# One 2 KB-row transfer for two blocks' filters, and a new table of places, in a long-convolution and SwiGLU kernel

## The chip, the core and the metric

The kernel runs on one core of a Trainium2 chip. The core has TensorE (PE, matmuls; its weight loads are shown as PEld), VectorE (DVE), ScalarE (ACT), GpSimd (POOL) and SyncE (SP, which here only issues transfers). They run side by side; each takes its own instructions strictly in the order in which the program issued them, and waits on semaphores for the others and for DMA transfers. The metric is the device time of one execution in microseconds.

## The reference

The sequence has 2048 rows of D = 640 channels, the feed-forward width is F = 1728, and everything is bf16 at the boundary.

```python
def _A_ref(q, k, v, shift_k, ssm_k, ssm_D):
    k_pad = jnp.pad(k, ((0, 0), (ks - 1, 0), (0, 0)))          # ks = 4
    for t in range(ks):                                        # four taps per channel
        k_shift = k_shift + k_pad[:, t:t + S, :] * shift_k[:, ks - 1 - t][None, None, :]
    kv = k_shift * v
    kv_f = rfft of kv over time, padded to 2 * S
    kf_f = rfft of ssm_k over time, padded to 2 * S            # ssm_k is (D, S)
    y = irfft(kv_f * kf_f)[:S]                                 # a causal convolution per channel
    y = y + kv * ssm_D[None, None, :]
    return q * y

def _B_ref(x, w_gate, w_up, w_down):
    return (silu(x @ w_gate) * (x @ w_up)) @ w_down

x = A_q
h = x + _A_ref(_layernorm(x), A_k, A_v, A_shift_k, A_ssm_k, A_ssm_D)
out = h + _B_ref(_layernorm(h), B_w_gate, B_w_up, B_w_down)
```

The fences above shorten the transforms to words.

## The kernel before

**Blocks.** Time is cut into NB = 4 blocks of BLK = 512 rows. Each block's piece of the filter `ssm_k` (called g) and of kv is carried into a spectrum by matmuls with a fixed basis (`forward`, weights WF). Spectra are called G0 to G3 and X0 to X3; each is of size "S" (two arena units: two halves `h` of four planes). From the G of a block and of the one before, `window` makes H (H0 = G0). The output spectrum A of block j is the sum of X_i times H_(j-i) over i = 0 to j (`mac`), so block 3 has four complex products, and an inverse transform (`inverse`, weights WI) brings it back to time. There follow the two layer norms, a transpose of the normalized rows (`turn_h`), and the feed-forward part (`ffn`): 13.5 chunks of 128 columns, gate and up projections of five matmuls each (`proj`, L769), Silu and products into `tT` (L783 to L787), and the down matmuls (L845). In the program of the order below, block j's convolution lies beside block j-1's feed-forward.

**mac in detail.** Where block j has more than one product, MODE is "one": each complex product needs four products of 128x2560 on VectorE (L542). Two of them are added into a buffer `acc`, two into the halves of A (through `plus`, L545). `acc` is one buffer, so its additions come one after the other. At the end come a subtraction and an addition (L581, L582), and then the inverse's own preparation (L662, L663, and L674, L677).

**Memory.** Blocks of 128 x 2560 bf16 live in an arena of 22 units of 5 KB per partition. A unit is given out at a buffer's first use and taken back after its last; a buffer of size 2 takes an even unit and its neighbour.

**What sets the order.** Every step is recorded as a numbered operation with an engine and its dependences, and then issued in the sequence of the table ORDER. A negative entry (the complement of the number) takes the operation's other form: an eviction of PSUM (L319, L413) goes to VectorE instead of ScalarE; a transfer from HBM (`load`) is issued from Pool's queue instead of SP's; an addition made by `added` is done not by VectorE but by an accumulating DMA that Pool issues (L243, the destination is read, added to and written by the transfer); the up half of a gate is read from PSUM directly by VectorE. Since buffers and arena units are given out in this sequence too, the table also sets which waits there are.

**g.** `load_g` brings the 512 time steps of one block, for 640 channels, as 128 x 5 x 512: rows of 1 KB. For block 0 the transposes are made by PE (L411) out of the loaded buffer; for blocks 1 to 3 ScalarE first rearranges the buffer by a copy (L419, 128x2560), and four transposing transfers from SP (L404) turn it.

The lines that the prediction speaks of:

```python
    def added(ns, fn, to, what, reads, write, n=1):
        plan.add("dve", ns, fn, reads, [write], ("add", 2 * P * R * D * n, lambda: nc.gpsimd.dma_start(out=to(), in_=what(), accum_op=ALU.add, max_dma_last_dim=4 * D)))
...
            dve(1402, lambda: v.tensor_sub(A.part(0), A.part(0), A.part(1)), [A.at(1)], [A.at(0)])
            dve(1402, lambda: v.tensor_add(A.part(1), total(), parts[1][0]()), [acc, parts[1][1]], [A.at(1)])
...
    act(400, lambda: nc.scalar.activation(ap(junk)[:, 0, 0:1], ap(bn)[:, 0, 0:1], ACT.Silu), [(bn, 0)], [])
```

The last of these (L871) is a Silu of one column, whose result isn't used; it is the first Silu of the program.

Of the kernel before, what the change touches and what calls it, by code (L numbers as in the profile page):

```python
# [16 lines left out]
D = 640  # L17
FF = 1728
P = 128
BLK = 512  # L20
NB = S_TOT // BLK
R = BLK // P
L = 2 * BLK
EPS = 1e-5
KT = D // P
# [166 lines left out]
def kernel(ctx: ExitStack, tc: tile.TileContext, A_q, A_k, A_v, A_shift_k, A_ssm_k, A_ssm_D, B_x,  # L192
# [21 lines left out]
    def new(kind):  # L214
        return Buf("U", kind, None, 2 if kind == "S" else 1) if kind in views else Buf(kind, kind)
# [66 lines left out]
    MB = P * R * D * 2  # L282
# [4 lines left out]
    def load_g(j):  # L287
        b = new("ld")
# [702 lines left out]
```

## Time and profile before

| | before |
|---|---|
| median of 3 runs | 251.36 us (251.21 to 253.07) |
| profiled execution: span | 251.4 us |
| TensorE busy | 237.3 us (94%) |
| VectorE busy | 197.7 us (79%) |
| ScalarE busy | 173.9 us (69%) |
| Pool busy | 54.0 us (21%) |
| bytes moved by DMA | 33.66 MB, mean 134 GB/s |
| accumulating transfers (L243) | 11 |

The profiled execution's own time is its span, 251.4 us; nothing lies outside of it. Busy time is the sum over an engine's instructions without the waits. A row of the chain of waits is start, length and what ran; a row of a timeline adds in brackets how long the engine was idle before it and who released it. In a row of windows, after the length, the engines stand in the order PE, PEld, DVE, ACT, POOL, each with busy time and count; then PE's granted clock, the share of the DMA engines that was busy, and GB/s.

### The profile page before, as it was taken

What the parts mean: (1) busy time and instruction counts of PE and PEld (TensorE: products, weight loads), DVE (VectorE), ACT (ScalarE), POOL (GpSimd) and SP (SyncE); (2) the same over time, 40 slices, a digit from 0 to 9 for tenths busy, and PEclk for the clock granted to TensorE, in tenths of its full rate; (3) what the DMA queues carried; (4) which work ended last, traced back from release to release, by engine and by line L of the source; (5) the groups of instructions that cost most, each with busy time, mean ns of one, the idle gap of its engine ahead of it and who ended that gap; (6) DMA issues with size and microseconds to landing.
All of it is one profiled execution on the core that took longest, in us unless ns stands there. A gap on an engine that the chain in (4) does not pass through costs nothing.

```text
span 251.4 us, 5138 instructions
## 1 busy us (share of the span) xinstructions
PE 237.3 (94%) x2113; PEld 153.0 (61%) x2125; DVE 197.7 (79%) x249; ACT 173.9 (69%) x300; POOL 54.0 (21%) x54
## 2 busy tenths in 40 slices
PE   3869997999999999999999999999999999999994
PEld 3447675788777677444465676454456785465662
DVE  2379999999999999999999989999999542131222
ACT  2449998999999976975988789983542865325100
POOL 0002003231540313220270404263612110000030
PEclk9999999999999999999999999999999999999999
DMA  5995699774998654685345468889592200000052
GB/s 156 376 212 163 127 324 352 231 197 92 165 246 292 202 81 81 105 154 133 79 66 146 86 99 194 148 146 163 98 224 29 26 0 3 0 0 3 0 78 78
DMA packets 37283, 33.66 MB, mean 134 GB/s; under 512 B 22470, under 2 KB 32076, under 8 KB 37260
## 3 DMA queue, kind: packets, MB, share of 16 engines
q1 hardware_dynamic: 31884, 21.38, 32.1%
q0 software_dynamic: 5376, 11.96, 25.9%
q8 instruction: 16, 0.26, 0.4%
q14 instruction: 7, 0.06, 0.1%
HBM read 16.29 MB, written 4.59 MB: 83 GB/s over the span
## 4 chain that ended last, share of the span: by engine, by line
PE 56%; ACT 17%; DMA 10%; DVE 9%; issue 4%; SPq 3%; DVEq 0%; ACTq 0%; POOLq 0%
PE ps L769 24%; PE ps L845 22%; ACT arena L319 7%; DMA arena<-in_A_ssm_k_dram 7%; PE ps L698 5%; DMA arena<-arena 3%; ACT sg L785 2%; PE ps L490 2%; SPq L404 2%; ACT junk L606 1%; PE ps L329 1%; PE ps L833 1%; DVE arena L674 1%; DVE arena L663 1%; DVE arena L662 1%
## 5 line engine op out<-in xcount | busy, mean ns | idle before, releaser
L769 PE MATMUL ps<-arena,wgu 128*128 128x512 bf16 (+1 forms) x668 | 116.7, 328 | 1.4 <-ACT sg L809 0.5
L769 PEld LDWEIGHTS <-wgu 128*128 128x128 bf16 x680 | 66.2, 98 | 45.3 <-issue 1.4
L845 PE MATMUL ps<-wd,tT 128*128 128x320 bf16 x416 | 59.1, 299 | 0.0
L845 PEld LDWEIGHTS <-tT 128*128 128x128 bf16 x416 | 39.8, 98 | 17.2 <-issue 1.8
L542 DVE TENSOR_TENSOR arena<-arena 128x2560 bf16<-128x2560 bf16 x30 | 44.1, 1484 | 0.2
L783 ACT ACTIVATE sg<-ps 128x1024 bf16<-128x1024 f32 (+1 forms) x28 | 26.9, 968 | 20.3 <-PE ps L769 19.7
L329 PE MATMUL ps<-arena,WF 128*128 128x320 bf16 x176 | 29.8, 299 | 1.2 <-ACT arena L319 0.9
L785 ACT CAST sg<-ps 128x1024 bf16<-128x1024 f32 (+1 forms) x23 | 23.0, 998 | 6.9 <-PE ps L769 3.1
L319 ACT CAST arena<-ps 128x320 bf16<-128x320 f32 (+1 forms) x48 | 25.2, 583 | 1.9 <-DVE arena L545 1.1
L610 POOL TENSOR_TENSOR sm<-sm,neghalf 128x4 f32<-128x4 f32 (+1 forms) x10 | 16.6, 1659 | 43.4 <-DVE sm L646 43.1
L787 DVE TENSOR_TENSOR tT<-sg,sg 128x1024 bf16<-128x1024 bf16 (+1 forms) x23 | 15.5, 673 | 11.5 <-ACT sg L785 11.5
L243 POOL DMA_DIRECT2D arena<-arena x11 | 13.3, 1211 | 47.4 <-DVE arena L542 11.2
L329 PEld LDWEIGHTS <-WF 128*128 128x128 bf16 x176 | 17.1, 98 | 10.0 <-issue 2.3
L606 ACT ACTIVATE junk<-arena 128x640 bf16<-128x640 bf16 x28 | 20.8, 744 | 1.3 <-DVE arena L709 1.3
L545 DVE TENSOR_TENSOR arena<-arena 128x2560 bf16<-128x2560 bf16 x14 | 20.7, 1487 | 0.2
L319 ACT ACTIVATE arena<-ps 128x640 bf16<-128x640 f32 (+1 forms) x32 | 20.2, 655 | 0.3
L698 PE MATMUL ps<-arena,WI 128*128 128x320 bf16 x96 | 15.7, 299 | 0.9 <-issue 0.6
L850 ACT ACTIVATE row<-ps,sm 128x640 bf16<-128x640 f32 x12 | 9.5, 791 | 8.2 <-PE ps L845 8.0
L709 DVE SCALAR_TENSOR_TENSOR arena<-arena,sm,ps 128x640 bf16<-128x640 bf16 x16 | 13.6, 876 | 1.8 <-ACT ps L707 1.8
L852 POOL DMA_DIRECT2D out_dram<-row x12 | 11.7, 1153 | 14.1 <-ACT row L850 14.1
L707 ACT ACTIVATE ps<-ps,sm 128x640 f32<-128x640 f32 x16 | 12.1, 770 | 3.7 <-PE ps L698 3.5
L698 PEld LDWEIGHTS <-WI 128*128 128x128 bf16 x96 | 9.0, 97 | 5.6 <-issue 1.3
(91 smaller groups left out, 240.8 us busy)
## 6 DMA issues: line engine op xcount, KB each, us to landing
arena<-arena POOLq DMA_DIRECT2D x11, 640.0 KB, 6.1
arena<-in_A_q_dram SPq DMA_DIRECT2D x4, 640.0 KB, 5.1
out_dram<-row POOLq DMA_DIRECT2D x13, 160.0 KB, 4.2
arena<-in_A_ssm_k_dram SPq DMA_DIRECT2D x3, 640.0 KB, 9.4
arena<-in_A_v_dram SPq DMA_DIRECT2D x3, 640.0 KB, 6.3
wd<-in_B_w_down_dram SPq DMA_DIRECT2D x2, 800.0 KB, 7.3
out_dram<-arena POOLq DMA_DIRECT2D x2, 640.0 KB, 5.8
wgu<-in_B_w_gate_dram SPq DMA_DIRECT2D x1, 800.0 KB, 6.5
```

The lines of the kernel that those rows point to most:

```text
L319: (lambda: nc.scalar.activation(dst(), src(), ACT.Copy, scale=2.0)) if twice else (lambda: nc.scalar.copy(dst(), src())),
L329: nc.tensor.matmul(ap(ps)[:, h, 0:NH], w, ap(src)[:, r, h * NH:(h + 1) * NH], start=(first and i == 0), stop=(last and i == len(rs) - 1), ...
L542: dve(1402, lambda: v.tensor_mul(to(), X.part(xs), H.part(hs)), [X.at(xs), H.at(hs)], [at])
L545: added(1402 * n - 69 * (n - 1), lambda: v.tensor_add(to(), to(), b()), to, b, [what], at, n)
L606: act(725, lambda r=r: nc.scalar.activation(waste(), ap(x)[:, r, :], ACT.Square, scale=D ** -0.5, accum_out=sm(s, MSQ, (r,))), [(x, r)], [ ...
L610: nc.gpsimd.tensor_tensor(sm(s, RSTD, rs), sm(s, VAR, rs), ap(neghalf)[:, 0:len(rs)], op=ALU.pow)
L698: nc.tensor.matmul(ap(ps)[:, w, 0:NH], m, src[:, w * NH:(w + 1) * NH], start=(i == 0), stop=(i == len(terms) - 1))
L769: nc.tensor.matmul(split(ap(ps), n)[:, i, :], w(k), ap(hT)[:, k, lo:lo + n], start=(k == 0), stop=(k == KT - 1))
L783: act(905 if wide_ else 490, lambda: nc.scalar.activation(of(sg), of(*gate), ACT.Silu), [(gate[0], gate[1] + i) for i in range(m)] + (psu ...
L785: op = plan.add("act", 905 if wide_ else 490, lambda: nc.scalar.copy(of(co), of(*up)), psu + [sg], [co] + tt, ("dve", 1135 if wide_ else 6 ...
L787: op.rest = dve(602 if wide_ else 336, lambda: nc.vector.tensor_mul(to(), of(sg), of(co)), [sg, co], tt)
L845: nc.tensor.matmul(ap(ps[hf])[:, hf, 0:NH], ap(tT)[:, c * BLK + at:c * BLK + at + P], ap(wd)[:, c, hf * NH:(hf + 1) * NH], start=False, st ...
```

## The change

`load_g(0)` now brings the g of blocks 0 and 1 in one transfer of 128 x 5 x 1024, whose rows are 2 KB, into a buffer of the new kind "pair", two neighbouring arena units. It returns a list of two pieces, each a buffer and a view of its half; block 1 takes the second piece and loads nothing. `g_turned` reads through that view. There is one operation fewer, so the numbers behind it shift by one, and the whole table ORDER is another.

```diff
-    0, 1, 2, 3, 16, 18, -20, 5, 4, 8, 17, 186, 9, 20, 22, 7, 10, 11, -22, 24, -26, 23, 26, 75, 76, 13, 15, 12, 6,
...
+    8, 16, 17, 26, 0, 1, 3, 9, 18, 19, 20, 10, 24, 7, 11, 5, -26, 22, 21, -24, 75, 12, 192, 6, 76, 36, 77, 78, 79,
...
+             "pair": ("p (c t) -> p c t", {"c": KT}), "scr": ("p (a d) -> p a d", {"a": 4}), "hT": ("p (k t) -> p k t", {"k": KT}),
...
-        return Buf("U", kind, None, 2 if kind == "S" else 1) if kind in views else Buf(kind, kind)
+        return Buf("U", kind, None, 2 if kind in ("S", "pair") else 1) if kind in views else Buf(kind, kind)
...
     def load_g(j):
-        b = new("ld")
-        load(MB, lambda q: q.dma_start(
-            out=ap(b).rearrange("p (c t) -> p c t", c=KT),
-            in_=A_ssm_k[0:D, j * BLK:(j + 1) * BLK].rearrange("(c p) t -> p c t", p=P)), [b])
-        return b
+        n = 2 if j == 0 else 1
+        b = new("pair" if n > 1 else "ld")
+        def at(i=0):
+            t = ap(b) if n > 1 else ap(b).rearrange("p (c t) -> p c t", c=KT)
+            return t[:, :, i * BLK:(i + 1) * BLK]
+        load(n * MB, lambda q: q.dma_start(
+            out=ap(b) if n > 1 else at(),
+            in_=A_ssm_k[0:D, j * BLK:(j + n) * BLK].rearrange("(c p) t -> p c t", p=P)), [b])
+        return [(b, lambda i=i: at(i)) for i in range(n)]
...
-    def g_turned(g, j):
+    def g_turned(loaded, j):
+        g, g_at = loaded
...
             act(2414, lambda: nc.scalar.copy(ap(by_r).rearrange("q a b -> q (a b)").rearrange("q (r c p) -> q r c p", r=R, c=KT),
-                                             ap(g).rearrange("q (c p r) -> q r c p", c=KT, r=R)), [g], [by_r])
+                                             g_at().rearrange("q c (p r) -> q r c p", r=R)), [g], [by_r])
...
-    gT = g_turned(g, 0)
+    gT = g_turned(g[0], 0)
...
-        g = load_g(j)
+        g = g[1:] or load_g(j)
...
-        gT = g_turned(g, j)
+        gT = g_turned(g[0], j)
```

What the table moves is seen in what each engine issues. At the start of the program SP and Pool issue the loads. SP before (`in_A_ssm_k_dram` is g, first of block 1, then of block 0; `in_A_q_dram` is x):

```order
L477 DMA arena<-in_A_k_dram 128x1280
L889 DMA arena<-in_A_shift_k_dram 5x512
L477 DMA arena<-in_A_k_dram 128x1280
L289 DMA arena<-in_A_ssm_k_dram 128x5x512
L296 DMA arena<-in_A_v_dram 128x2560
L903 DMA WF<-const_wf 128x1024
L904 DMA arena<-in_A_ssm_D_dram 1x640
L289 DMA arena<-in_A_ssm_k_dram 128x5x512
L903 DMA WF<-const_wf 128x1024
L301 DMA arena<-in_A_q_dram 128x2560
```

Pool before issued no transfer there. Now SP has these, the last a transpose of block 1's g that waits for ScalarE's copy:

```order
L895 DMA arena<-in_A_shift_k_dram 5x512
L483 DMA arena<-in_A_k_dram 128x1280 x2
L301 DMA arena<-in_A_v_dram 128x2560
L294 DMA arena<-in_A_ssm_k_dram 128x5x1024
L409 DMA_TRANSPOSE arena<-arena 128x5x128
```

and Pool, behind the identity matrix, these:

```order
L878 AFFINE_SELECT ident<-ident 128x128
L909 DMA WF<-const_wf 128x1024
L910 DMA arena<-in_A_ssm_D_dram 1x16x40
L306 DMA arena<-in_A_q_dram 128x2560
L909 DMA WF<-const_wf 128x1024
L752 DMA wd<-in_B_w_down_dram 128x3x640
L915 DMA WI<-const_wi 128x1024
L301 DMA arena<-in_A_v_dram 128x2560
L755 DMA wd<-in_B_w_down_dram 64x640
L294 DMA arena<-in_A_ssm_k_dram 128x5x512
```

The pair stands fifth on SP, and WF, x and others have moved to Pool's queue, beside it. ScalarE's first instructions before (L419 is the copy of block 1's g, L319 an eviction of block 0's first transform):

```order
L871 ACT_TABLE_LOAD
L871 ACTIVATE junk<-bn 128x1
L413 COPY kT<-ps_75 128x5x128
L419 COPY arena<-arena 128x2560
L413 COPY arena<-ps_73 128x640
L319 ACTIVATE arena<-ps_72 128x320
```

and now (L425 is the copy, L324 the eviction, L877 the Silu of one column):

```order
L418 ACT_TABLE_LOAD
L418 COPY kT<-ps_73 128x5x128
L418 COPY kT<-ps_74 128x5x128
L425 COPY arena<-arena 128x2560
L324 ACTIVATE arena<-ps_74 128x320
L877 ACT_TABLE_LOAD
L877 ACTIVATE junk<-bn 128x1
L324 ACTIVATE arena<-ps_75 128x320
```

The Silu stands behind the first eviction, with a second table load of its own, and the eviction of a g transpose (L413, 128x640) is gone from ScalarE. The third place is Pool's queue in block 3, ahead of its inverse, with the semaphores waited for (a DMASW one is a transfer that Pool issued, a DMAHW one a transfer of SP). Before, with the load of v and one layer norm's small work between:

```order
L243 DMA arena<-arena 128x2x1280 [waits DMASW4_49,DMASW2_49,DVE_49]
L243 DMA arena<-arena 128x2x1280 [waits DMASW5_49,DVE_49]
L243 DMA arena<-arena 128x2x1280 [waits DVE_49]
...
L243 DMA arena<-arena 128x2x1280 [waits DMASW5_49]
L243 DMA arena<-arena 128x2x1280 [waits DMASW3_49,DMASW0_49,DVE_49]
L852 DMA out_dram<-row_68 128x640 [waits DMAHW4_49,DMASW1_49]
L243 DMA arena<-arena 128x2x1280 [waits DMASW6_49,DVE_49]
```

Now (L858 adds a row of the feed-forward's result to the output; a second such row is left out):

```order
L243 DMA arena<-arena 128x2x1280 [waits DMASW5_49,DVE_49,PE_49]
L243 DMA arena<-arena 128x2x1280 [waits DMASW6_49,DVE_49]
L243 DMA arena<-arena 128x2x1280 [waits DMASW7_49,DMASW5_49]
L858 DMA out_dram<-row_67 128x640 [waits DMASW0_49,Activation_49]
L243 DMA arena<-arena 128x2x1280 [waits DMAHW5_49,DMAHW6_49,DMAHW1_49,DMAHW7_49,DMAHW0_49,DMASW1_49]
L243 DMA arena<-arena 128x2x1280 [waits DMASW6_49,DMASW2_49,DVE_49]
L243 DMA arena<-arena 128x2x1280 [waits DMAHW2_49,DMAHW3_49,DMASW7_49,DMASW3_49]
...
L243 DMA arena<-arena 128x2x1280 [waits DMASW3_49,DVE_49]
L243 DMA arena<-arena 128x2x1280 [waits DMASW1_49,DVE_49]
L243 DMA arena<-arena 128x2x1280 [waits DMASW5_49]
L243 DMA arena<-arena 128x2x1280 [waits DMASW6_49,DMASW0_49,DVE_49]
L243 DMA arena<-arena 128x2x1280 [waits DMASW7_49,DVE_49]
```

Eleven accumulating transfers stand where six stood, all eleven behind the spectrum G3; five of them wait for an earlier one's landing on `acc`. In the whole program there are 25 instead of 11, and VectorE has 14 additions fewer. On VectorE the addition L588 (L582 before) now waits for the last of the eleven, and two products into tT (L793), L668, L669 and L680 (L662, L663, L674 before) stand around and behind it ahead of block 3's inverse.

More of the change, by code (lines that the diff above doesn't have):

```diff
@@ L201 @@
     views = {"x": ("p (r d) -> p r d", {"r": R}), "t4": ("p (r d) -> p r d", {"r": R}), "ld": (None, None), "early": (None, None),
-             "scr": ("p (a d) -> p a d", {"a": 4}), "hT": ("p (k t) -> p k t", {"k": KT}),
+             "pair": ("p (c t) -> p c t", {"c": KT}), "scr": ("p (a d) -> p a d", {"a": 4}), "hT": ("p (k t) -> p k t", {"k": KT}),
              "minus": ("p (a q) -> p a q", {"a": 5}), "S": ("p (h a d) -> p h a d", {"h": 2, "a": 4})}
@@ L425, in g_turned @@
             for r in range(R):
-                transposed(lambda c, r=r: ap(g).rearrange("q (c p r) -> q c p r", c=KT, r=R)[:, c, :, r], [g],
+                transposed(lambda c, r=r: g_at().rearrange("q c (p r) -> q c p r", r=R)[:, c, :, r], [g],
                            lambda r=r: ap(gT)[:, r, :].rearrange("p (c q) -> p c q", c=KT), (gT, r))
```

82 rows, old and new, of the table ORDER are left out of this document.

## The prediction

> **What bounds the kernel now.** I read the page first, then the windows, the chain of waits, and single groups.
>
> ```profile
> span 251.4 us, 5138 instructions
> PE 237.3 (94%) x2113; PEld 153.0 (61%) x2125; DVE 197.7 (79%) x249; ACT 173.9 (69%) x300; POOL 54.0 (21%) x54
> ```
>
> TensorE (PE) is busy in all but 14.1 us. The windows say where those lie (length, then busy time of PE, PEld, VectorE, ScalarE, Pool, then PE's granted clock, DMA share, GB/s).
>
> ```profile
> 0.00:5.00 5.00, 1.00 (x11) 0.80 (x12) 0.42 (x3) 1.49 (x2) 0.54 (x6) 1.00 0.52 153
> 5.00:10.00 5.00, 4.91 (x130) 3.62 (x129) 2.23 (x8) 1.28 (x2) 0.00 (x0) 1.00 0.89 317
> 10.00:15.00 5.00, 2.02 (x36) 0.83 (x35) 3.15 (x6) 1.91 (x1) 0.00 (x0) 1.00 1.40 373
> 20.00:30.00 10.00, 10.00 (x74) 6.96 (x72) 9.85 (x18) 10.00 (x28) 1.88 (x2) 1.00 0.56 116
> 30.00:40.00 10.00, 9.25 (x194) 6.18 (x193) 9.79 (x16) 9.40 (x21) 0.66 (x1) 1.00 1.00 305
> 40.00:50.00 10.00, 8.74 (x75) 6.82 (x74) 9.54 (x16) 9.07 (x18) 2.70 (x2) 1.00 0.88 281
> 60.00:70.00 10.00, 9.46 (x87) 8.21 (x85) 10.00 (x10) 9.91 (x22) 5.08 (x2) 1.00 0.83 148
> 130.00:140.00 10.00, 9.66 (x65) 5.92 (x65) 9.90 (x14) 8.69 (x15) 0.56 (x1) 1.00 0.46 101
> 240.00:252.00 12.00, 7.95 (x59) 5.18 (x57) 2.87 (x4) 0.00 (x0) 1.86 (x3) 1.00 0.39 82
> ```
>
> Half of it, 15 - 7.93 = 7.1 us, is the start; 2.0 lies in 30 to 50, 0.9 in 60 to 70 and 130 to 140, and of the last window's 4.05 some 3.4 lie behind the last matmul (251.4 - 247.98, the last row below). That is 13.4 of 14.1, so little is left elsewhere. The chain of waits (start, length, what) agrees.
>
> ```profile
> 3.90 11.01 DMA arena<-in_A_ssm_k_dram
> 14.96 1.03 PE ps L411 x15
> 17.87 4.15 ACT arena L319 x12
> 82.20 7.17 PE ps L845 x52
> 163.35 1.08 PE ps L769 x5
> 194.60 1.09 PE ps L698 x8
> 247.98 0.55 DVE row L864
> ```
>
> PE waits for g of block 0 until 14.96, then ScalarE's evictions (L319) set the pace, and from about 50 us PE runs densely. PE takes its instructions in a fixed order, so a new table can win at most some 1.4 us after 50 us; but wherever PE comes to an inverse transform before VectorE has its input ready, the wait is lost in full.
>
> **The change part by part.** The profiled execution's span, 251.4, is its own time, and the median of the runs is 251.36; sums start from 251.4. Lines are those of before; in the changed kernel they stand 5 or 6 further down.
>
> *The start.* Rows of 2 KB: should they lift the 1.31 MB of g from the 317 GB/s of 5 to 10 us to the 373 of 10 to 15, they save 0.6 us; at worst nothing. What travels beside them matters more. SP now issues k, v and the pair (2.62 MB); Pool issues, with no wait ahead, both halves of WF, x, part of the down weights, half of WI and v of block 1 (2.6 MB). If SP's bytes went first, the pair would land near 10.4: 0.77 MB by 5 us at 153 GB/s, the other 1.85 MB at the mean of 345. If a Pool byte goes beside each SP byte, 5.24 MB are through at about 18. In the first three windows 4.2 MB had moved when g landed at 14.9. I take 16, some 1 later: two queues with like bytes are nearer to the second case. By the Trainium skill (DMA: Bandwidth & Descriptors, "Queues, rings and completion order") each DMA engine takes turns, packet by packet, between the queues that have work; by that the pair lands at the late end, and the sum would be 2 us higher. No run here has the two queues full together.
>
> ```profile
> 0.79 1.28 ACT L871 ACT_TABLE_LOAD   x1 [0.79 <-PEq L975]
> 2.08 0.20 ACT L871 ACTIVATE junk<-bn 128x1 bf16<-128x1 f32 x1
> 9.41 2.50 ACT L419 COPY arena<-arena 128x2560 bf16<-128x2560 bf16 x1 [2.57 <-DMA arena<-in_A_ssm_k_dram]
> 16.30 1.37 ACT L319 ACTIVATE arena<-ps 128x320 bf16<-128x320 f32 x3
> 55.55 2.59 ACT L419 COPY arena<-arena 128x2560 bf16<-128x2560 bf16 x1
> ```
>
> ScalarE's copy of g of block 1 (2.50) lay at 9.41, where ScalarE was idle. Now it waits for the pair and stands ahead of the first eviction, which came 1.34 behind g's landing and now comes 2.5 behind it: 1.2 later. The warm-up Silu is moved behind that eviction, and a second table load stands there: 1.28 + 0.20 in a stretch in which ScalarE is soon 10.00 of 10 busy. Three evictions of some 0.5 (1.37 / 3) go to VectorE, -1.5. The copy for block 2, at 55.55, now stands ahead of the first inverse: +2.6, less the transforms of 1.4 us that PE can do there. ScalarE's sum is at most +3.7, and at least 0 if PE has buffers enough ahead; I take +1 of it. With the pair 1 later and 0.5 won by the rows and by evictions that run side by side, the start gives **+1.5**. Its ends: -3.0 (all of PE's idle time between 10 and 15 gone, 5 - 2.02) and +6 (the pair at 18, ScalarE's evictions in full).
>
> *Accumulating transfers.* The new table makes 25 additions by a Pool DMA that adds (L243), where 11 were; 14 additions of 1.48 us leave VectorE (the price of the like-shaped L542 below). The price of a transfer:
>
> ```profile
> L243 POOL DMA_DIRECT2D arena<-arena x11: 1177/1197/1277, 51.3 to 178.5; - x11
> DMA to landing us min/median/max: 5.7/6.1/8.1
> 153.25 1.19 POOL L243 DMA_DIRECT2D arena<-arena  x1 [0.90 <-DVE arena L542]
> 156.11 1.19 POOL L243 DMA_DIRECT2D arena<-arena  x1 [1.67 <-DVE arena L537]
> 142.00:144.00 2.00, 2.00 (x17) 1.46 (x16) 1.86 (x4) 1.35 (x4) 1.09 (x1) 1.00 1.09 196
> 157.00:161.00 4.00, 3.95 (x22) 1.84 (x20) 4.00 (x5) 4.00 (x9) 0.30 (x1) 1.00 1.05 188
> ```
>
> One alone (142 to 144) takes the DMA engines whole: a share of 1.09 at 196 GB/s. With two in flight (157 to 161), the rate is 188. So they don't overlap: each of 655 KB takes 655 / 192 = 3.4 us of all the engines, and what is queued behind it waits. The last of a queue lands 5.7 - 3.4 = 2.3 later than its bytes began to move out. The bounds for one are 3.4 (queued) and 5.7 (one after the other).
>
> *Block 1.* Five accumulates follow each other, and VectorE's last addition ahead of the inverse (L582) waits for them: 5 x 3.4 + 2.1 = 19.1. Between the subtraction that allows the first and that addition VectorE has six products, one of double length, three products into tT and small work of 2.2:
>
> ```profile
> L542 DVE TENSOR_TENSOR arena<-arena 128x2560 bf16<-128x2560 bf16 x30 | 44.1, 1484 | 0.2
> 152.99 2.83 DVE L537 TENSOR_TENSOR arena<-arena 128x5120 bf16<-128x5120 bf16 x1
> 161.66 0.68 DVE L787 TENSOR_TENSOR tT<-sg,sg 128x1024 bf16<-128x1024 bf16 x1
> 189.05 1.49 DVE L662 TENSOR_TENSOR arena<-arena 128x2560 bf16<-128x2560 bf16 x1
> 192.10 1.56 DVE L674 TENSOR_TENSOR arena<-arena 128x1280 bf16<-128x1280 bf16 x2
> 151.39 1.11 PE ps L490 x112
> ```
>
> 6 x 1.47 + 2.83 + 3 x 0.67 + 2.2 = 15.8 (back to back, an instruction costs the 44.1 / 30 of the group). VectorE waits 19.1 - 15.8 = 3.3, and PE, dense here, waits as long: **+3**, between 0 (VectorE was late anyway, by the 14 additions it is rid of) and +5. In block 2 six accumulates stand at the same place, with four more products of 1.47 beside them: 3.3 + 3.4 - 5.9 = 0.8, less than the margin of these estimates: 0.
>
> *Block 3.* This is the largest term. Behind G3's last forward VectorE needs an eviction (0.6), five operations of 1.47 and small ones (0.8), 8.6 in all, before the first accumulate can go. All eleven go between it and the inverse, six of them into one buffer (acc), where each waits until the one before has landed. With three row transfers of a quarter of the bytes (0.85 each) they take 11 x 3.4 + 3 x 0.85 + 2.3 = 42.3. Then L582 waits for the last, and in order behind it stand two products into tT (0.67), the inverse's L662 and L663 (1.49) and half of L674 (0.78): 1.47 + 1.34 + 2.98 + 0.78 = 6.6, with a few gaps 6.9. Sum 57.8. In the same stretch PE has 27 projections (1.08), 119 down matmuls and 16 of transforms (7.17 / 52 = 0.138), and the taps (1.11 + 0.4): 29.2 + 18.6 + 1.5 = 49.3. So PE is done 8.5 us before its inverse. If the transfers cost only their latency one after the other on acc, six times 5.7, the sum is 8.6 + 34.2 + 6.9 = 49.7, and PE waits 0.4. The row nearest to eleven in queue is that of 157 to 161, which had two and was already at the plateau; I take **+6**, nearer to the plateau than to the bare latency, since some of the five others can pass while acc waits for a landing.
>
> The Trainium skill (DMA: Bandwidth & Descriptors, "Anatomy of one DMA — SWDGE (gpsimd) path") has about 2.0 us and bytes / 436 GB/s for one transfer of this kind, 3.5 us here by my estimate; six on acc would be 21 us and PE would wait nowhere. The trace disagrees: 5.7 at the least.
>
> *Relief.* VectorE has 14 x 1.47 = 20.6 us less to do, and what PE lost between 60 and 200, at most 1.4, may go: **-1**.
>
> Sum: 251.4 + 1.5 + 3 + 6 - 1 = 260.9, about 261.
>
> **The rivals.** *A: VectorE's relief and an early pair win.* SP's bytes go first, the pair lands near 11, PE's wait of 3 is gone, and the accumulates hide. For it: SP's 2.62 MB are less than the 4.2 that had moved when g landed. Against: ScalarE's three additions to the start, and the plateau at 190 GB/s. 251.4 - 3 + 1 - 1 = 248.4, about 248.
>
> *B: the accumulates are hidden*, because the five that are not on acc fill the gaps between landings. It decides in block 3, if the last accumulate lands within 49.3 - 6.9 = 42.4 us of G3's last forward, and likewise in block 1. For it: the bare latency in block 3 gives a wait of 0.4. Against: 8.6 and the bytes' 37.4 alone are 46. 251.4 + 1.5 - 1 = 251.9, about 252. The time by the Trainium skill's sum for one transfer, above, would be this one.
>
> *C: a worse start, no stalls.* The pair lands at 18 (+3.1) and ScalarE's sum counts nearly in full, with the rest as in B: 251.4 + 6 - 0.5 = 256.9, about 257. It decides once Pool's transfers take half of the DMA engines in the first 15 us. That is what the Trainium skill's rule on turns between the queues, above, would make of the start.
>
> That the change doesn't do what it says can be left out: the order shows one load of 128x5x1024 and 25 accumulates.
>
> **How the numbers follow.** The main case has 0.58: 261, from 255 (block 3 at +1, block 1 at 0 and the start at +3) to 267 (the start at +3, block 1 at +4, block 3 at +8.5). A has 0.12, B 0.20, C 0.10. About 1% is what a measurement of this kernel tells from no change, 248.9 to 253.9. Faster is A, 0.12; the same is B, 0.20; slower is the main case and C, 0.68. The range goes from 250.5, which takes in B, to 267, and leaves out A and the ends of the main case.
>
> **What would show it.** In the changed profile the pair's DMA (out of in_A_ssm_k) lands at about 16; the second ACT_TABLE_LOAD lies behind the first eviction; L243 stands 25 times with a median over 6 us to landing; the windows of block 3 show about 190 GB/s over some 35 us; VectorE's busy time falls to about 177, and it idles ahead of L588 on a DMA; PE has two gaps ahead of the inverse (L698 before) of about 3 in block 1 and 6 in block 3. Wrong would be: no gap ahead of block 3's inverse (B), a pair before 12 (A), or a PE idle time that grows mostly before 50 us (C).

## The result and the profile after

The changed kernel takes 305.38 us (median of 4 runs, 301.86 to 307.40), against 251.36 (251.21 to 253.07). Two of the four, 306.63 and the profiled one of 307.40, fell in a slow state, so the ratio goes by the other two, whose mean is 303.0: 1.204, 95% interval 1.197 to 1.211. It is slower by some 51 us, where 9.6 were forecast. The time of an execution is 1.7 us longer than its span here (307.40 and 305.7), so the span of 251.4 before most likely belongs to the execution of 253.07, and something does lie outside of it; below, spans are compared with spans and times with times. The page of the changed kernel:

```profile
span 305.7 us, 5152 instructions
PE 253.8 (83%) x2114; PEld 159.2 (52%) x2125; DVE 189.4 (62%) x248; ACT 164.0 (54%) x284; POOL 75.5 (25%) x83
```

PE's idle time has gone from 251.4 - 237.3 = 14.1 us to 305.7 - 253.8 = 51.9, which is 37.8 of the 54.3 between the two spans; the other 16.5 are in PE's busy time itself, for the same matmuls. The largest waits of PE, one row for each line and releaser (total, times, longest), show how the idle time is made up:

```profile
PE ps L775 <- DMA arena<-row: 8.3, 1, 8.3
PE ps L416 <- DMA arena<-in_A_ssm_k_dram: 7.0, 1, 7.0
PE ps L496 <- DMA kT<-in_A_k_dram: 4.3, 2, 4.2
PE ps L839 <- ACT sg L791: 4.3, 1, 4.3
PE ps L775 <- DVE tT L792: 3.8, 1, 3.8
PE ps L775 <- DMA wgu<-in_B_w_gate_dram: 3.7, 1, 3.7
PE ps L775 <- ACT sg L791: 3.5, 1, 3.5
PE ps L775 <- DVE arena L327: 3.5, 1, 3.5
```

They are in essence eight single waits at eight places, with seven different releasers, and none is longer than 8.3. None of them is at an inverse transform, where the prediction had its gaps: the page's row of the inverse's matmuls (count, busy time, mean ns, idle time ahead) has no idle time.

```profile
L704 PE MATMUL ps<-arena,WI 128*128 128x320 bf16 x96 | 17.1, 322 | 0.0
```

PE stops at projections and down matmuls ahead of the inverse instead, for instance where the buffers that they need wait for products of VectorE. What the waits do to the busy time is seen in the windows (length, PE, PEld, VectorE, ScalarE, Pool, PE's granted clock, DMA share, GB/s):

```profile
12.00:19.40 7.40, 0.69 (x3) 0.10 (x1) 0.00 (x0) 0.00 (x0) 0.00 (x0) 0.73 0.94 330
19.40:24.00 4.60, 4.35 (x54) 3.39 (x55) 2.79 (x7) 3.85 (x3) 0.00 (x0) 0.50 0.13 28
36.00:42.00 6.00, 1.68 (x35) 0.83 (x33) 5.97 (x8) 2.65 (x6) 0.00 (x0) 0.78 1.15 252
42.00:46.00 4.00, 4.00 (x23) 2.19 (x16) 2.60 (x4) 3.84 (x5) 0.00 (x0) 0.50 0.88 306
96.00:100.00 4.00, 4.00 (x20) 2.75 (x19) 3.86 (x5) 2.45 (x5) 0.57 (x1) 0.50 0.36 76
236.00:241.00 5.00, 3.26 (x14) 1.91 (x15) 4.97 (x7) 1.20 (x2) 0.00 (x0) 0.53 0.00 0
```

After seven of the eight waits PE runs for some 3 to 6 us at a clock of 0.50. The 16.5 us by seven are 2.4, so that a wait of 4 us costs about 6. In the profile before, the clock was 1.00 throughout. The Trainium skill (TensorE: Matmul & The Clock Gate, "Part 1: The HAM clock gate") has it that one idle window of about 3.4 us brings the half clock, and one busy window takes it away. These two traces agree for the most part: the wait of 2.98 us in the kernel before left the clock at 1.00, and those of 3.5 to 8.3 here didn't, except the one of 3.7 at 68 us. A later run doesn't: with the new sequence and the old engines, the clock was at 0.50 after single waits of 2.0 to 2.8 us as well (after one of 2.3 at 118 us, for instance). So no length of a wait that leaves the clock alone is shown.

The first matmul of each inverse transform cuts the time into stages:

| first matmul of | before, us | after, us | stage before | stage after | stage longer by |
|---|---|---|---|---|---|
| inverse of block 0 | 28.7 | 43.1 | 28.7 | 43.1 | 14.4 |
| inverse of block 1 | 75.6 | 99.6 | 46.9 | 56.5 | 9.6 |
| inverse of block 2 | 133.0 | 158.3 | 57.4 | 58.7 | 1.3 |
| inverse of block 3 | 194.4 | 240.4 | 61.4 | 82.1 | 20.7 |
| (end of the span) | 251.4 | 305.7 | 57.0 | 65.3 | 8.3 |

The stages don't hold the same work as before. Counted by matmuls, the stage of block 2 has lost 140 taps, 30 forward matmuls and 24 projections of 512 columns to other stages; that of block 3 has gained 28 forward matmuls and 26 such projections and has passed 52 down matmuls on to the end. By the times that rows of before give for one (7.17 us for 52 down matmuls, 10.14 for 47 projections of 512 columns), I estimate the work of the stages at full clock as 1 us more in block 0, 1 less in block 1, 9 less in block 2, 2 more in block 3 and 7 more at the end. For the same work the stages are therefore longer by some 13, 11, 10, 19 and 1. The loss is spread over all four blocks. The chain of waits (start, length, what) names what holds the stages up:

```profile
2.59 17.01 DMA arena<-in_A_ssm_k_dram
34.86 6.85 DMA kT<-in_A_k_dram
67.58 7.45 DMA arena<-arena
80.35 10.45 DMA arena<-arena
123.90 8.97 DMA arena<-row
200.72 10.45 DMA arena<-arena
224.95 7.02 DMA arena<-arena
```

The pair lands at 19.6, block 1's transposes of k at 41.7, and accumulating transfers stand in the chain of blocks 1 and 3. Behind the last of them, at 231.97, the chain goes on through VectorE to the down matmuls ahead of the inverse:

```profile
233.47 0.68 DVE tT L793
237.74 2.85 PE ps L851 x10
240.59 1.21 PE ps L704 x8
```

The group of the accumulating transfers:

```profile
L243 POOL DMA_DIRECT2D arena<-arena x25: 1179/1194/2045, 47.1 to 225.0; - x25
DMA to landing us min/median/max: 5.7/7.0/11.3
```

### The profile page after: what moved, and what is told of

It reads as the page before. It is cut to its first block, busy times and chain, and to the rows that moved or that the text cites. A ratio compares the mean times of both kernels' runs of the same rounds, so it can differ in the third digit from the quotient of the medians.

```text
span 305.7 us, 5152 instructions
## 1 busy us (share of the span) xinstructions
PE 253.8 (83%) x2114; PEld 159.2 (52%) x2125; DVE 189.4 (62%) x248; ACT 164.0 (54%) x284; POOL 75.5 (25%) x83
## 4 chain that ended last, share of the span: by engine, by line
PE 41%; DMA 28%; issue 10%; ACT 8%; DVE 6%; POOL 4%; SPq 2%; POOLq 0%; DVEq 0%; ACTq 0%
PE ps L775 19%; DMA arena<-arena 18%; PE ps L851 10%; DMA arena<-in_A_ssm_k_dram 6%; PE ps L704 5%; PE ps L334 5%; DMA arena<-row 3%; POOL sm L616 2%; DMA kT<-in_A_k_dram 2%; ACT junk L612 2%; ACT arena L324 2%; SPq L409 2%; PE ps L416 1%; ACT junk L635 1%; DVE arena L548 1%
## 5 line engine op out<-in xcount | busy, mean ns | idle before, releaser
L775 PE MATMUL ps<-arena,wgu 128*128 128x512 bf16 (+1 forms) x669 | 124.0, 341 | 24.6 <-DMA arena<-row 8.3
L851 PE MATMUL ps<-wd,tT 128*128 128x320 bf16 x416 | 61.0, 303 | 1.7 <-DVE tT L793 1.7
L548 DVE TENSOR_TENSOR arena<-arena 128x2560 bf16<-128x2560 bf16 x30 | 44.1, 1487 | 17.8 <-DMA arena<-arena 17.7
L243 POOL DMA_DIRECT2D arena<-arena x25 | 31.3, 1274 | 84.3 <-DVE arena L548 29.7
L789 ACT ACTIVATE sg<-ps 128x1024 bf16<-128x1024 f32 (+1 forms) x28 | 26.8, 966 | 19.1 <-PE ps L775 18.2
L791 ACT CAST sg<-ps 128x1024 bf16<-128x1024 f32 (+1 forms) x19 | 18.4, 967 | 31.4 <-DVE tT L793 14.7
L334 PE MATMUL ps<-arena,WF 128*128 128x320 bf16 x176 | 31.9, 319 | 0.9 <-DVE arena L327 0.4
L616 POOL TENSOR_TENSOR sm<-sm,neghalf 128x4 f32<-128x4 f32 (+1 forms) x10 | 15.8, 1576 | 48.9 <-DVE sm L652 48.6
L324 ACT CAST arena<-ps 128x320 bf16<-128x320 f32 (+1 forms) x45 | 23.3, 576 | 2.1 <-PE ps L334 1.9
L612 ACT ACTIVATE junk<-arena 128x640 bf16<-128x640 bf16 x28 | 20.6, 739 | 1.4 <-DVE arena L715 1.3
L793 DVE TENSOR_TENSOR tT<-sg,sg 128x1024 bf16<-128x1024 bf16 (+1 forms) x19 | 12.5, 659 | 11.5 <-ACT sg L791 11.4
L324 ACT ACTIVATE arena<-ps 128x640 bf16<-128x640 f32 (+1 forms) x26 | 16.1, 644 | 5.9 <-PE ps L334 5.7
L858 POOL DMA_DIRECT2D out_dram<-row x12 | 12.9, 1263 | 14.5 <-ACT row L856 14.5
L792 DVE TENSOR_TENSOR tT<-sg,ps 128x1024 bf16<-128x1024 bf16 (+1 forms) x9 | 9.9, 1101 | 10.5 <-ACT sg L789 6.6
L713 ACT ACTIVATE ps<-ps,sm 128x640 f32<-128x640 f32 x16 | 11.9, 768 | 6.0 <-PE ps L704 5.8
L425 ACT COPY arena<-arena 128x2560 bf16<-128x2560 bf16 x3 | 7.7, 2557 | 13.4 <-DMA arena<-in_A_ssm_k_dram 13.4
```

The costliest lines, as they stand in the source:

```text
L324: (lambda: nc.scalar.activation(dst(), src(), ACT.Copy, scale=2.0)) if twice else (lambda: nc.scalar.copy(dst(), src())),
L334: nc.tensor.matmul(ap(ps)[:, h, 0:NH], w, ap(src)[:, r, h * NH:(h + 1) * NH], start=(first and i == 0), stop=(last and i == len(rs) - 1), ...
L548: dve(1402, lambda: v.tensor_mul(to(), X.part(xs), H.part(hs)), [X.at(xs), H.at(hs)], [at])
L612: act(725, lambda r=r: nc.scalar.activation(waste(), ap(x)[:, r, :], ACT.Square, scale=D ** -0.5, accum_out=sm(s, MSQ, (r,))), [(x, r)], [ ...
L616: nc.gpsimd.tensor_tensor(sm(s, RSTD, rs), sm(s, VAR, rs), ap(neghalf)[:, 0:len(rs)], op=ALU.pow)
L775: nc.tensor.matmul(split(ap(ps), n)[:, i, :], w(k), ap(hT)[:, k, lo:lo + n], start=(k == 0), stop=(k == KT - 1))
```

## The experiments

Thirteen kernels were run; they are told in the order in which one led to the next. An entry of ORDER that is negative, -n, is operation n - 1 in its other form, so that taking it back writes n - 1.

**All 25 additions back on VectorE.**

```diff
-    ... -218, ... -251, ... -254, ... -262, ... -441, ... -684, ... -699, ...
+    ... 217, ... 250, ... 253, ... 261, ... 440, ... 683, ... 698, ...
```

> The changed kernel with all 25 accumulating transfers turned back into additions on VectorE, at the same places of the table. Theory: PE's gaps of 9 us (60 to 100), 8.5 us (120 to 134), 3.6 (190 to 200) and 9.6 us (220 to 240), and the half clock that follows each of them, are waits for these transfers; the gaps go, VectorE takes 25 x 1.48 = 37 us more and stays under the span, and the time falls by 30 to 40 us, to 265 to 275; what is left over 251 is the start. Rival: the table's order on PE comes to the inverses too early whoever adds (VectorE, now 226 us busy, becomes the bound); then the gaps stay, and the time is above 285.

It took 297.25 us, some 6 less than the changed kernel (303.0). The rival held: in 80 to 230 us VectorE is now busy 9.9 to 10.0 of 10 almost everywhere, and the four inverses begin at 41.6, 98.2, 154.8 and 230.1. The gaps went to other releasers: with the transfers gone, PE's places are still too early. VectorE has 223.0 us of busy time here, 33.6 more, so this run doesn't price the transfers by themselves.

**The start's loads on SP.**

```diff
-    ... 12, ... -15, ... -16, ... -28, ... -14, ... -184, ... -30, ... -191, ... -186, ... -409, ...
+    ... 12, 14, 13, 15, ... 27, ... 183, ... 29, ... 190, ... 185, ... 408, ...
```

> The changed kernel with the nine loads of the start issued by SP instead of Pool, both halves of WF right behind the pair. Theory: the pair landed at 19.6 because Pool's packets of 4 to 5 KB took turns with its packets of 2 KB; alone in one queue it lands at 11 to 13, PE's gap of 7 us falls under 3, the clock stays 1.00 in 20 to 30, and the time falls by 6 to 9 us, to 296 to 299. Rival: the pair is late by its own size; it lands after 17 and the time stays within 2 us of 305.

It took 304.88 us. The landing went as the theory had it: block 0's g no longer holds PE up, and the first forward matmul starts at 12.7 instead of 21.9. The time didn't follow: the inverse of block 0 starts at 42.2, 0.9 sooner. Two rows of PE's timeline (start, length, what, and in brackets the wait ahead and its releaser) show the next wait in line, longer than the 4.2 before:

```profile
24.86 0.43 PE L334 MATMUL ps<-arena,WF 128*128 128x320 bf16 x2 [3.08 <-DVE arena L327]
40.30 0.42 PE L496 MATMUL ps<-diag,kT 32*128 32x128 bf16 x12 [7.66 <-DMA kT<-in_A_k_dram]
```

What the theory says of the queues is seen in the changed kernel itself. Its DMA view for 9 to 16 us (queue, packets, MB, share of the engines), with Pool's queue as q0 and SP's as q1:

```profile
q0 software_dynamic: 450, 1.80, 65.9%
q1 hardware_dynamic: 448, 0.92, 35.0%
```

One packet of SP's for one of Pool's, 450 to 448, but two bytes of Pool's for one of the pair's, because Pool's packets have 4.0 KB on the mean here and the pair's 2. The rule of the Trainium skill that the prediction cites (DMA: Bandwidth & Descriptors, "Queues, rings and completion order") is that queues take turns by packet. The trace agrees for these rows, and the bytes are shared by the size of a row. It doesn't give such a count for the transposes of k: from 31 to 35 us SP's queue moved 1040 packets of some 250 bytes and Pool's 113, so there it wasn't one for one.

**The pair with the old table.** The load of the pair at the place of block 0's g, block 1's load taken out, and all numbers above it lower by one.

> One part alone: the table of the kernel before, with the pair loaded at the place of block 0's g and the load of block 1's g taken out. Theory: the bytes ahead of the pair's end are the same, so it lands at 14 to 15; ScalarE's copy of block 1's g now lies ahead of its first evictions and costs about 1 us; the time is 251 to 253, and the whole loss is the table's. Rival: rows of 2 KB are much faster, the pair lands before 13 and the time is 249 or less; or the two neighbouring units make waits elsewhere in the arena and the time is above 256.

It took 270.77 us (ratio 1.076, 1.066 to 1.085). The theory failed; the second rival, waits elsewhere in the arena, had this. In the old table the load of v comes after k has been used up, and without block 1's g in the arena it gets k's unit. The waits of SP's queue (its first two rows for this line):

```profile
SPq L300 <- DMA arena<-in_A_k_dram: 3.2, 1, 3.2
SPq L300 <- PE ps L415: 1.3, 1, 1.3
```

The chain of waits has the pair's load (issue, time to landing):

```profile
7.74 8.57 DMA arena<-in_A_ssm_k_dram
```

SP waits there with the pair's own load behind it, which is issued at 7.74 instead of 3.90. Further on, SP waits 9.4 us for a unit ahead of block 1's transposes. So this run doesn't price the pair but its places in the arena: a change of one buffer's size moved the units of others, and the queue is held up where a unit isn't free.

**The pair undone, the new table kept.**

```diff
-    ... 26, ... 12, ...
+    ... 26, 12, 186, ...
```

> The pair undone, the new table kept: g of block 0 and g of block 1 by two transfers of 1 KB rows, one behind the other on SP at the pair's place. Theory: queues take turns by packets, so 640 packets for block 0's g take about as long as the 640 larger ones of the pair did: it lands at 17 to 18.5, block 1's g at 20 to 22; the pair itself costs nothing, and the time is 303 to 309. Rival: the pair is what delays the start; block 0's g lands at 14 or before, the inverse of block 0 begins at 38 or before, and the time falls below 299.

It took 318.83 us, which neither theory had. g of block 0 lands at 15.1 and that of block 1 at 16.9, sooner than forecast, since here Pool's load of block 1's v waits for a unit (16.9 us in the waits of its queue), and no longer travels beside them. But that load, block 2's g and others come later, and beside block 1's transposes, which PE waits for:

```profile
33.85 0.45 PE L329 MATMUL ps<-arena,WF 128*128 128x320 bf16 x2 [4.16 <-DMA arena<-arena]
42.38 1.78 PE L329 MATMUL ps<-arena,WF 128*128 128x320 bf16 x6 [3.15 <-DMA arena<-arena]
```

In each table the other way of loading g was the slower one (318.83 against 303.0 here, 270.77 against 251.6 in the old table). Neither run isolates what 2 KB rows are worth; that stays open.

**A longer warm-up.**

```diff
-WARM = 9
+WARM = 32
```

> The changed kernel with 32 instead of 9 warm-up matmuls, which reach over the wait for the pair from 12.3 to 19.4. Theory: the half clock of 19.4 to 25 follows from PE's idle time just before; with PE busy the clock stays 1.00 there, PE's 54 instructions of 19.4 to 24 take half the time, and the time falls by 2 to 3 us, to 302 to 303.5 on the median of 305.4, while the half clock behind the other gaps stays. Rival: the clock falls for another reason (power, DMA load): it is 0.5 there again and the time is the same.

It took 308.13 us. The clock of 19.4 to 24 us went as the theory had it (the windows, columns as above):

```profile
19.40:24.00 4.60, 3.65 (x58) 2.54 (x59) 3.75 (x10) 4.26 (x4) 0.00 (x0) 1.00 0.10 23
```

The timeline of PE in the same run has the next wait:

```profile
44.96 0.43 PE L496 MATMUL ps<-diag,kT 32*128 32x128 bf16 x12 [8.78 <-DMA kT<-in_A_k_dram]
```

The clock is 1.00 instead of 0.50, with 58 instructions in 3.65 us instead of 54 in 4.35. The half clock of this place does come from PE's own idle time. But PE only arrived sooner at its next wait, which grew from 4.2 to 8.8 us. Two loads of weights went out on Pool 1.5 us sooner here, at 29.3 and 30.3, ahead of most of k's transposes; that they are the reason is argued, not shown.

**More loads on SP.** As in the second run, and four more loads of weights there too.

```diff
-    ... -182, ... -178, ... -174, ... -185, ...
+    ... 181, ... 177, ... 173, ... 184, ...
```

> The run with the start's loads on SP, and four more loads of weights (two of them issued by Pool at 30.8 and 31.7 us) on SP too, behind the transposes of kT. In the earlier run g landed 8 us sooner, but PE then waited 7.7 us for block 1's kT transposes, and the inverse of block 0 began at 42.2 all the same (28.7 before). Theory: those transposes move in packets of 256 bytes and take turns with Pool's packets of 4.6 and 5 KB; without these they land by about 33, the gap falls under 2 us, the inverse of block 0 begins at 34 to 37, the gap of 4 us at 68 goes too, and the time falls by 7 to 12 us, to 293 to 298. Rival: the transposes are late by SP's own queue, the inverse of block 0 stays at 40 or later, and the time within 3 us of 305.

It took 299.4 us, the median of 296.94 and 301.87: some 4 to 6 less than the changed kernel, at the late end of the forecast. The wait for k's transposes is gone, and the inverse of block 0 starts at 37.2. That it isn't sooner lies at block 1's g, whose transposes PE awaits: 

```profile
26.34 0.71 PE L334 MATMUL ps<-arena,WF 128*128 128x320 bf16 x2 [3.95 <-DMA arena<-arena]
```

**Loads on Pool in the kernel before.** The same choice put into the old table.

```diff
-    ... 13, 15, ... 14, ... 27, ... 28, ... 29, ... 192, ...
+    ... -14, -16, ... -15, ... -28, ... -29, ... -30, ... -193, ...
```

> The kernel before, its own table and its two loads of g, with seven loads of the start (both halves of WF, the skip row, x of block 0, both halves of WI, v of block 1) issued by Pool instead of SP. Theory: packets of 4 to 5 KB on Pool's queue take turns with g's packets of 1 KB and hold block 0's g back although its bytes ahead are fewer: it lands at 14 to 17 instead of 14.9 or sooner, block 1's kT transposes land later than 31.4, and the time is 252 to 262. Rival: Pool's queue only relieves SP; g lands at 12 or before, WF with it, and the time is 249 to 251.

It took 259.45 us (ratio 1.029, 1.023 to 1.036). The time is in the forecast range, and g of block 0 lands at 18.3, still later than forecast, with 1 KB rows, where the bytes ahead of it on SP were fewer than before. The inverse of block 0 starts at 34.0 instead of 28.7, and the stages behind it are as long as before. The wait of 4.60 us ahead of g's transposes is the only new long one there (PE's timeline), and the clock of 10 to 30 us falls to 0.79 and 0.87:

```profile
18.34 1.79 PE L411 MATMUL ps<-ident,arena 128*128 128x128 bf16 x15 [4.60 <-DMA arena<-in_A_ssm_k_dram]
```

This prices these seven loads on the second queue at 7.4 us in the old table.

**Five of block 3's transfers back on VectorE.**

```diff
-    ... -683, ... -688, ... -684, ... -691, ... -699, ...
+    ... 682, ... 687, ... 683, ... 690, ... 698, ...
```

> The changed kernel with five of block 3's eleven accumulating transfers done by VectorE, so that the same six additions are on Pool as in the kernel before. From the inverse of block 2 to that of block 3 it took 82.1 us, and 61.4 before, though 7 us of PE's work stand behind it now. Theory: the chain of transfers is what is late; with six of them this stretch is 66 to 72 us and the time falls by 10 to 16, to 289 to 295. Rival: VectorE itself comes too late, because the table puts block 3's products behind too much other work (with all additions on VectorE the stretch took 75.3); then it stays at 75 to 82 and the time falls by less than 7.

It took 302.59 us, no change that can be told from the changed kernel's 303.0, and the stage of block 3 took 78.4 instead of 82.1: the rival. PE's wait of 3.8 for a product into tT is gone, and the one behind the last addition, 4.3 in the changed kernel, is longer:

```profile
230.79 0.69 PE L839 MATMUL ps<-wd,tT 64*128 64x320 bf16 x3 [5.37 <-ACT sg L791]
```

**Eleven transfers in block 3 of the kernel before.** The counterpart in the old table, five additions more on Pool.

```diff
-    ... 683, ... 684, ... 688, ... 691, ... 699, ...
+    ... -684, ... -685, ... -689, ... -692, ... -700, ...
```

> The kernel before, with its own table, and eleven instead of six of block 3's additions made by accumulating transfers: the same eleven as in the changed kernel. Theory: 11 x 3.4 us and the waits on acc do not fit ahead of its inverse; PE gets a gap of 6 to 15 us there, the clock falls behind it, and the time is 258 to 270. Rival: the transfers are hidden (VectorE is rid of 7 us); the time is within 2 us of 251.4.

It took 278.83 us (ratio 1.102, 1.089 to 1.115), above the forecast. The inverse of block 3 starts at 220.2 instead of 194.4. Four rows of the chain of waits (start, length, what):

```profile
166.41 5.83 DMA arena<-arena
183.98 8.45 DMA arena<-arena
192.72 5.96 DMA arena<-arena
199.94 9.70 DMA arena<-arena
```

And two of PE's timeline:

```profile
197.10 6.21 PE L769 MATMUL ps<-arena,wgu 128*128 128x512 bf16 x15 [10.12 <-ACT sg L785]
211.81 1.78 PE L845 MATMUL ps<-wd,tT 128*128 128x320 bf16 x6 [5.30 <-DVE tT L787]
```

The first is issued at 154.7 and the last lands at 209.6: 54.9 us, 5.0 for each of the eleven, where I had 3.4. In that time the DMA engines were busy to 0.84 only. Pool takes its instructions in order; one that waits for a landing on acc keeps back those that don't. And VectorE, waiting for the last, keeps back products into tT that have nothing to do with it (the 5.30); ScalarE then has no buffer for its next eviction and PE none for its next projection (the 10.12).

**Both repairs together.** All loads of the first 70 us on SP, the additions split about as before.

> The changed kernel with both repairs: all loads of the first 70 us on SP, as in the run before it (299.4), and the additions of blocks 1 to 3 split between Pool and VectorE as in the kernel before (10 on Pool). Theory now: queues and transfers are only a part of the loss, and the places of PE's work in the table are the rest: the two repairs give 6 and 3 to 8 us, and the time is 288 to 297, still 36 us or more above 251. Rival: both waits covered for each other, and with both gone the table is as good as the old one: below 270.

It took 289.64 us: the theory. Together the repairs give some 13 us, more than tried apart, but this run takes 15 additions back where that above took five. 38 us over the kernel before remain.

**The halves of the table apart.** First the old sequence with the new choices of engine.

> The two halves of the table apart, first one: the old sequence of operations, with the new table's choice of engine for each (the 82 negative entries: 25 accumulating transfers, loads on Pool, evictions on VectorE), and block 0's and block 1's g by two loads. Theory: both halves are bad by themselves and the losses cover each other, since a wait that is there anyhow hides another. The engines alone bring the loads on Pool (7 us when tried alone) and eleven transfers in block 3 (27 us when tried alone): 280 to 300. Rival: the new choices only hurt at the new places; below 265.

It took 358.98 us (ratio 1.419, 1.400 to 1.438), far above the forecast. Its largest new waits:

```profile
POOL arena L243 <- DMA arena<-arena: 39.0, 7, 8.8
DVE arena L542 <- DMA arena<-arena: 32.7, 8, 8.3
DVE arena L581 <- DMA arena<-arena: 21.1, 3, 9.2
```

Then the new sequence with the old choices.

> The other half: the new sequence with the pair, and the old table's choice of engine for each operation (36 negative entries, 11 of them transfers that add, no load of the start on Pool); both halves of WF stand right behind the pair. Theory: PE's places alone are 30 us or more too early for VectorE and for the transposes: 278 to 295, with the inverses of blocks 0, 1, 2, 3 at about 36, 87, 144 and 215 to 223, as in the run with both repairs. Rival: what was left there were the evictions moved to VectorE, which this run takes back too; below 265.

It took 292.75 us, as the theory had it, with the inverses at 35.9, 87.6, 142.0 and 224.9, the last a little later than forecast. The largest waits of PE are smaller than in the changed kernel:

```profile
PE ps L333 <- ACT arena L323: 7.4, 9, 2.3
PE ps L774 <- ACT sg L788: 5.1, 1, 5.1
PE ps L774 <- DMA arena<-row: 4.1, 2, 2.3
PE ps L495 <- ACT sg L790: 2.8, 1, 2.8
```

PE's busy time in this run:

```profile
PE 251.4 (87%) x2125; PEld 156.8 (54%) x2125; DVE 198.0 (68%) x249; ACT 175.8 (61%) x301; POOL 50.7 (17%) x54
```

It is 14.1 us more than before, again with a clock of 0.50 after waits, and the idle time is 24.4 us more. The stage of block 3 takes 82.9 us, with six accumulating transfers, where the changed kernel takes 82.1 with eleven: in the new sequence it is late whoever adds. So the new sequence (with both halves of WF moved forward) costs 40 us with the pair and with the old engines. The new engines cost 106 in the old sequence, but only some 10 more in the new one.

**A version that might be faster: block 0's g first, in the kernel before.**

```diff
-    ... 17, 186, 9, ... 13, 15, 12, 6, ... 193, ... 14, ...
+    ... 17, 12, 9, ... 13, 15, 14, 186, 6, ... 91, 193, ...
```

> The kernel before with block 0's g loaded ahead of block 1's (their places in the table exchanged), the second half of WF ahead of block 1's g, ScalarE's copy of block 1's g behind its seventh eviction, and block 2's g loaded 12 places earlier so that the arena has room. Theory: PE's wait for g of block 0 (2.98 us up to 14.96) goes, since it lands at about 9.4; the first forward matmul comes at 12.5 to 13.5 instead of 15.8, and 1 to 3 us stay: 248.4 to 250.4. Rival: ScalarE sets the pace to 50 us, and takes the 2.5 us of the copy into its full stretch: the time is 251 to 253.

It took 257.58 us (ratio 1.021, 1.016 to 1.025), worse than the theory and the rival. The first forward matmul came at 14.4 instead of 15.8, but ScalarE's copy of 2.5 us now lies among its evictions, and later loads are issued later:

```profile
20.23 0.43 PE L329 MATMUL ps<-arena,WF 128*128 128x320 bf16 x2 [1.82 <-ACT arena L319]
50.36 1.81 PE L769 MATMUL ps<-arena,wgu 128*128 128x256 bf16 x15 [2.20 <-DMA wgu<-in_B_w_gate_dram]
```

No version tried here beats the kernel before.

## Why the prediction was wrong

The sign was right; the size was not, and 305 lies far outside the range. Of the signs named, 25 transfers with a median of 7.0 us to landing and the second table load are there; the pair at 19.6, VectorE's 189.4 us of busy time, and the lack of a gap at any inverse are not as forecast. By the steps of the prediction, with the stages counted for the same work:

**The start, +1.5; measured some 13 up to the inverse of block 0.** The step "I take 16" failed: the pair landed at 19.6, later than even the late end of 18. I had shared the DMA engines by bytes, while from 9 to 16 us they were shared by packets, and Pool's were twice as large. The rule stood in the prediction, cited for a landing at 18, but I worked it out for equal packets. Rival C had this mechanism. ScalarE's part was right: the copy runs from 19.62, the first eviction comes at 22.67, 3.1 behind the landing where 2.5 were forecast, and the second table load of 1.28 lies behind it. What I had not looked at is the rest of the stage: PE's row for block 1's taps now stands ahead of block 0's inverse, and their transposes move in small packets beside Pool's large ones; PE waits 4.2 us for them. The two waits put some 4 us more into PE's busy time by the half clock.

**Block 1, +3; measured some 11.** Five transfers were taken at 19.1; they ran from 67.58 to 90.80, 23.2, with a load of 640 KB of weights, issued by Pool just ahead of them, beside them. PE met this as a wait of 3.5 at a projection. To that come a wait of 3.7 for weights that Pool loaded late, and the half clock at 96.

**Block 2, 0; measured some 10.** The stage as it stands is 1.3 longer, but it has 9 us less of PE's work, so this 0 is wrong too. PE has its longest wait here, 8.3 us, for transposes of rows that landed late (8.97 in the chain) beside accumulating transfers, and 5 us at half clock behind it. The sum had only VectorE's path to the inverse, not PE's other rows.

**Block 3, +6; measured some 19.** The path was the one forecast: L588 starts at 232.06, when the last transfer has landed, and products into tT, L668, L669 and half of L680 stand behind it ahead of the inverse at 240.38. PE's work beside it was right as well (49.0 us at full clock by my estimate, 49.3 forecast). The length of the path was not: from the end of G3's last forward (171.6) it took 68.8 us, not 57.8. The first transfer came 11.9 behind that forward, not 8.6. The eleven transfers were taken at 42.3; they took from 183.54 to the landing of the last at 231.97, 48.4. The engines were busy to 0.99 in that time, at 180 GB/s, and moved 8.71 MB, where eleven transfers and three rows are 7.7: the rate was nearly as forecast, and what failed is the step that only three rows move beside them. (In the old table it was the waits in Pool's queue: 54.9, with the engines busy to 0.84.) Behind the last landing it took 8.4, not 6.9. PE did not wait at the inverse but at projections and down matmuls, 13.5 us in all in this stretch, and ran at half clock behind these waits. Yet the transfers alone don't explain the stage: with five of them on VectorE the time is the same, and with the old engines the stage is as long.

**Relief, -1; measured nothing.** VectorE's busy time fell by 8.3 us, not by 20.6, since the table also moves evictions and products to it (82 negative entries against 36, all kinds together). I had counted three of these.

**What failed above all** is a step that isn't a term: that PE, dense before, stays dense except at the two or three places that I worked out. The new sequence alone, with every engine as before, costs 40 us. The sum had no term for that, and none for the half clock: 16.5 us of the 54 between the spans lie in PE's busy time, close to half as much again as the 37.8 of idle time.

Shown are the sharing by packets between the pair's rows and Pool's, the price of seven loads on the second queue (7.4 us in the old table), of five more transfers (26 us, in the old table too), of the sequence with the pair (40 us), and, at one place, that the half clock follows PE's idle time. Not shown is which places of the sequence make up the 40: the waits in that run are many, 5.1 us at the longest, for ScalarE's evictions, for transfers and for VectorE's products. What the pair by itself is worth stays open too.

## What to carry to other kernels

Where an engine is dense, a new order is priced at all of its waits, not at the ones that come to mind: go through what each row on the dense engine now stands ahead of, and ask when that is ready. Add to PE's idle time about half as much again for the clock: it was 16.5 us on 37.8 here, and 14.1 on 24.4 with the old engines. Compare stages only for the same work. Rows of 2 KB in one queue got half the bytes of rows of 4 KB in the other, so a load that an engine waits for should not travel beside large rows that nobody waits for.

## What the runs showed of the hardware

- Two queues shared the DMA engines packet for packet: 450 of Pool's and 448 of SP's in 7 us, with 1.80 and 0.92 MB. For transposes in small packets it was 1040 of SP's to 113 of Pool's in 4 us.
- Seven of eight waits of PE from 3.5 to 8.3 us were followed by a granted clock of 0.50 for 3 to 6 us, one of 3.7 was not. One of 2.98 us in the kernel before left it at 1.00, and one of 2.3 with the new sequence and the old engines did not. A warm-up that covered a wait of 7.0 kept it at 1.00.
- Eleven accumulating transfers of 655 KB on one queue, six of them into one buffer, took 48 and 55 us, 4.4 and 5.0 each, where 3.4 is what one needs of the DMA engines by the 192 GB/s of the kernel before. In the first case the engines were busy to 0.99, with other transfers beside them; in the second to 0.84.
